# Mirror values by subtraction on VectorE and GpSimd in two of three steps, in place of a sixth product on TensorE

## Chip, cores and metric

One core of one Trainium2 chip. The metric is the device time in microseconds (us) of one execution. Medians are of 4 to 11 runs.

Engines: PE is TensorE, DVE is VectorE, ACT is ScalarE, POOL is GpSimd, SP starts most DMAs.

## The reference

A two-dimensional Fourier transform (real part only) of 8 sequences of 3008 x 256, then a gated feed-forward layer:

```python
X = np.fft.fft(x, axis=1)
X = np.fft.fft(X, axis=2)
x = X.real.astype(np.float32).reshape(B * S, D)       # 24064 x 256
gate = np.maximum(x @ w_gate, 0.0)                    # 256 x 1536
val = x @ w_val
return (gate * val @ w_out).astype(np.float32)
```

The kernel never builds the last axis of the transform: it multiplies the folded cosine and sine tables into the weights, so that a row of the transform and its mirror image share products.

## The kernel before

The work is 288 steps: 8 batches, 3 blocks of rows in each, 12 slices of 128 hidden features. For one slice, `pq[:, 0]` is the even part of the input and `pq[:, 1]` the odd part. With weights `wc` and `ws` a step makes the gate `G` and the value `V` of 512 rows. A further product with `wm` then turns each of them, in place in PSUM, into the gate and value of the 512 mirror rows. `wm` is -2 times `ws`, except in row 0, where it is 0, because that row holds a term that does not change sign. So a step has six products of 512 columns, of which two, one for `G` and one for `V`, only make the mirror rows.

```python
def plus(b, blk, f, i):            # i = 0: gate, i = 1: value
    ...
    nc.tensor.matmul(e[i][:], lhsT=wc[i][:, fs], rhs=pq[:, 0, :], start=True, stop=False)
    nc.tensor.matmul(e[i][:], lhsT=ws[i][:, fs], rhs=pq[:, 1, :], start=False, stop=True)
    if i == 0:
        e["gs"] = gp.tile([128, 512], F32, tag="gs", name="gs")
        nc.scalar.activation(e["gs"][:], e[0][:], ACTF.Relu)
    else:
        nc.vector.tensor_tensor(e["h"][:, 0, :], e["gs"][:], e[1][:], op=ALU.mult)

def minus(b, blk, f, i):
    ...
    nc.tensor.matmul(e[i][:], lhsT=wm[i][:, fs], rhs=pq[:, 1, :], start=False, stop=True,
                     skip_group_check=True)
    ...                            # gate: Relu on ScalarE; value: mirror half of h = gs * V on VectorE

for t in range(n + NF):
    for i in range(2):
        if 0 < t <= n:
            minus(*steps[t - 1], i)
        if t < n:
            plus(*steps[t], i)
    for fn in extra.get(t, ()):    # pieces of the next batch's transform, loads, folds
        fn()
    if t >= NF:
        out_piece(*steps[t - NF])  # eight output products of 256 columns
```

The "folds" are GpSimd's: they add and subtract the halves of the input of the batch after next. The issue order of each engine is the program's order.

## Time and profile before

| | before |
|---|---|
| time, median | 734.13 us |
| step without transform pieces | 2.17 us |
| from one batch to the next | 81.32 us |
| busy: PE, DVE, ACT, POOL | 92%, 63%, 52%, 30% |
| TensorE clock granted | 0.998 |

Lines of the page of the kernel before: the span; the busy us, share and instructions of each engine; the chain of waits followed back from the last instruction, as shares of the span; and three groups, each with its line, engine, operation, output<-input, shapes and count, then busy us and mean ns of one, then the idle time in front of it and who ended most of it.

```profile
span 733.5 us, 12121 instructions
...
PE 676.0 (92%) x4354; PEld 432.3 (59%) x4432; DVE 462.5 (63%) x747; ACT 381.8 (52%) x701; POOL 221.5 (30%) x116
...
PE 87%; DMA 4%; POOL 3%; DVE 3%; issue 1%; ACT 1%; SPq 0%; POOLq 0%; ACTq 0%; DVEq 0%
...
L367 DVE TENSOR_TENSOR h<-gs,V 128x512 bf16<-128x512 f32 x288 | 197.9, 687 | 215.5 <-PE V L360 161.2
...
L353 DVE TENSOR_TENSOR h<-gs,V 128x512 bf16<-128x512 f32 x288 | 195.9, 680 | 1.1 <-ACT gs L351 0.5
...
L360 PE MATMUL V<-pq,wm_92 128*128 128x512 bf16 x288 | 109.4, 380 | 4.2 <-DVE h L353 3.9
```

The chain is 87% PE. The two VectorE groups are the products gate times value of the plain rows (line 353) and of the mirror rows (line 367). The third group, 288 products into V with `wm`, is the one that the change attacks. PE's groups add up to more than its busy time, because matmuls overlap; distances between starts are the better measure. The timeline of one step (start us, duration us, engine, line, operation, count; other engines' lines and weight loads left out):

```profile
451.86 0.38 PE L360 MATMUL G<-pq,wm_91 128*128 128x512 bf16 x1
...
452.08 0.38 PE L347 MATMUL G<-pq,wc_87 128*128 128x512 bf16 x1
...
452.30 0.38 PE L348 MATMUL G<-pq,ws_89 128*128 128x512 bf16 x1
...
452.51 0.38 PE L360 MATMUL V<-pq,wm_92 128*128 128x512 bf16 x1
...
452.73 0.38 PE L347 MATMUL V<-pq,wc_88 128*128 128x512 bf16 x1
...
452.94 0.38 PE L348 MATMUL V<-pq,ws_90 128*128 128x512 bf16 x1
...
453.00 0.69 DVE L367 TENSOR_TENSOR h<-gs,V 128x512 bf16<-128x512 f32 x1 [0.92 <-PE V L360]
453.16 1.04 PE L385 MATMUL po<-wo,h 128*128 128x256 bf16 x8
...
454.03 0.38 PE L360 MATMUL G<-pq,wm_91 128*128 128x512 bf16 x1
```

A 512-column product starts every 0.21 to 0.22 us, eight output products take 0.87 us (453.16 to 454.03), and the step from one mirror gate product to the next is 454.03 - 451.86 = 2.17 us. PE has no gap. Below, "step" always means this distance.

### The profile page before, as it was taken

The numbers are of one execution on the slowest core, as the hardware profiler recorded it, in microseconds if no ns is written. First come the engines' busy times: TensorE is split into PE (matmuls) and PEld (weight loads), VectorE is DVE, ScalarE is ACT, GpSimd is POOL, SyncE is SP. The second block draws the span as 40 slices with busy tenths as digits, with TensorE's granted clock in tenths as the row PEclk, the third lists the DMA queues.
The fourth block names the chain that finished last, engine by engine and source line by source line (L and its number), as shares of the span: only waits on it lengthen the run. The fifth ranks groups of instructions, "written<-read, shape, count | busy, mean of one in ns | idle before, by whom it ended". The sixth has DMA issues, their size and how long they took to land.

```text
span 733.5 us, 12121 instructions
## 1 busy us (share of the span) xinstructions
PE 676.0 (92%) x4354; PEld 432.3 (59%) x4432; DVE 462.5 (63%) x747; ACT 381.8 (52%) x701; POOL 221.5 (30%) x116
## 2 busy tenths in 40 slices
PE   0168899899999999999999999999999999999997
PEld 0033366566666666666666666666666666666665
DVE  6613766566666766666666667666666667666661
ACT  2114555456555555555555555555555655555551
POOL 2836829202920086004910095005900000000000
PEclk9999999999999999999999999999999999999999
DMA  9467172616342544216251554135221151111213
GB/s 200 169 153 130 42 163 74 155 30 160 101 114 59 119 117 99 71 43 175 72 137 36 119 143 109 35 84 144 64 57 29 30 142 28 44 44 28 56 30 84
DMA packets 26971, 67.61 MB, mean 92 GB/s; under 512 B 3856, under 2 KB 17680, under 8 KB 24720
## 3 DMA queue, kind: packets, MB, share of 16 engines
q1 hardware_dynamic: 24340, 51.84, 27.2%
q0 software_dynamic: 2448, 13.37, 8.2%
q10 hardware_dynamic: 124, 1.64, 1.0%
q8 instruction: 34, 0.56, 0.3%
q14 instruction: 25, 0.20, 0.1%
HBM read 36.68 MB, written 30.93 MB: 92 GB/s over the span
## 4 chain that ended last, share of the span: by engine, by line
PE 87%; DMA 4%; POOL 3%; DVE 3%; issue 1%; ACT 1%; SPq 0%; POOLq 0%; ACTq 0%; DVEq 0%
PE po L385 34%; PE G L348 9%; PE V L360 9%; PE G L360 8%; PE V L347 8%; PE V L348 8%; PE G L347 7%; DMA Td<-t_256 2%; DVE h L353 1%; DMA t_969<-Td 1%; DMA t_304<-Td 1%; DMA Td<-t_719 1%; DVE q L37 0%; POOL xl L89 0%; POOL q L35 0%
## 5 line engine op out<-in xcount | busy, mean ns | idle before, releaser
L367 DVE TENSOR_TENSOR h<-gs,V 128x512 bf16<-128x512 f32 x288 | 197.9, 687 | 215.5 <-PE V L360 161.2
L364 ACT ACTIVATE gs<-G 128x512 f32<-128x512 f32 x288 | 172.2, 598 | 242.0 <-PE G L360 242.0
L385 PE MATMUL po<-wo,h 128*128 128x256 bf16 x2304 | 297.1, 273 | 0.4
L385 PEld LDWEIGHTS <-h 128*128 128x128 bf16 x2304 | 222.8, 98 | 64.5 <-issue 2.4
L353 DVE TENSOR_TENSOR h<-gs,V 128x512 bf16<-128x512 f32 x288 | 195.9, 680 | 1.1 <-ACT gs L351 0.5
L351 ACT ACTIVATE gs<-G 128x512 f32<-128x512 f32 x288 | 171.1, 594 | 0.8 <-PE G L348 0.8
L88 POOL TENSOR_TENSOR xc<-xl,xh 94x3840 f32<-94x3840 f32 (+1 forms) x8 | 60.6, 7572 | 291.0 <-DMA xl<-in_x_dram 274.7
L360 PE MATMUL V<-pq,wm_92 128*128 128x512 bf16 x288 | 109.4, 380 | 4.2 <-DVE h L353 3.9
L348 PE MATMUL G<-pq,ws_89 128*128 128x512 bf16 x282 | 107.1, 380 | 2.9 <-issue 0.2
L360 PE MATMUL G<-pq,wm_91 128*128 128x512 bf16 x288 | 109.4, 380 | 0.4 <-ACT gs L351 0.3
L347 PE MATMUL V<-pq,wc_88 128*128 128x512 bf16 x288 | 109.4, 380 | 0.0
L348 PE MATMUL V<-pq,ws_90 128*128 128x512 bf16 x267 | 101.4, 380 | 0.0
L347 PE MATMUL G<-pq,wc_87 128*128 128x512 bf16 x237 | 89.8, 379 | 0.0
L89 POOL TENSOR_TENSOR xl<-xl,xh 94x3840 f32<-94x3840 f32 (+1 forms) x8 | 60.6, 7579 | 0.6
L347 PEld LDWEIGHTS <-wc_88 128*128 128x128 bf16 x288 | 28.2, 98 | 40.0 <-issue 7.5
L391 ACT COPY os<-po 128x512 f32<-128x512 f32 x48 | 28.1, 585 | 40.6 <-PE po L385 40.6
L348 PEld LDWEIGHTS <-ws_90 128*128 128x128 bf16 x288 | 28.2, 98 | 34.2 <-issue 0.3
L348 PEld LDWEIGHTS <-ws_89 128*128 128x128 bf16 x288 | 28.2, 98 | 34.0 <-issue 0.3
L360 PEld LDWEIGHTS <-wm_92 128*128 128x128 bf16 x288 | 28.2, 98 | 34.0 <-issue 0.3
L117 PEld LDWEIGHTS <-w_82 94*96 94x96 bf16 x120 | 15.7, 131 | 50.3 <-issue 28.0
L389 DVE COPY os<-po 128x512 f32<-128x512 f32 x48 | 33.0, 688 | 6.7 <-PE po L385 6.7
L347 PEld LDWEIGHTS <-wc_87 128*128 128x128 bf16 x288 | 28.2, 98 | 5.2 <-issue 0.8
(345 smaller groups left out, 346.3 us busy)
## 6 DMA issues: line engine op xcount, KB each, us to landing
out_dram<-os SPq DMA_DIRECT2D x176, 128.0 KB, 2.1
xl<-in_x_dram SPq DMA_DIRECT2D x7, 1360.0 KB, 9.8
xl<-in_x_dram SPq DMA_DIRECT2D x7, 238.0 KB
wst_103<-in_moe_w_gate_dram SPq DMA_DIRECT2D x2, 768.0 KB, 19.6
wst_106<-in_moe_w_val_dram SPq DMA_DIRECT2D x2, 768.0 KB, 22.9
out_dram<-os SPq DMA_DIRECT2D x16, 96.0 KB, 5.2
xl<-in_x_dram ACTq DMA_DIRECT2D x1, 1360.0 KB
Td<-t_256 SPq DMA_DIRECT2D x4, 192.0 KB, 9.1
```

Of the source, the lines that this page charges most:

```text
L88: eng.tensor_tensor(c1, x1, rev, op=ALU.subtract)
L89: eng.tensor_tensor(x1, x1, rev, op=ALU.add)
L347: nc.tensor.matmul(e[i][:], lhsT=wc[i][:, fs], rhs=pq[:, 0, :], start=True, stop=False)
L348: nc.tensor.matmul(e[i][:], lhsT=ws[i][:, fs], rhs=pq[:, 1, :], start=False, stop=True)
L351: nc.scalar.activation(e["gs"][:], e[0][:], ACTF.Relu)
L353: nc.vector.tensor_tensor(e["h"][:, 0, :], e["gs"][:], e[1][:], op=ALU.mult)
L360: nc.tensor.matmul(e[i][:], lhsT=wm[i][:, fs], rhs=pq[:, 1, :], start=False, stop=True, skip_group_check=True)
L364: nc.scalar.activation(e["gs"][:], e[0][:], ACTF.Relu)
L367: nc.vector.tensor_tensor(free(e["h"][:], 512 + NB - 1, [NB, 16], [-1, NB]), e["gs"][:].rearrange("p (a k) -> p a k", k=NB), e[1][:].rearr ...
L385: nc.tensor.matmul(po[:, s % 2, :], lhsT=ht[b, blk, ff][:, sg, g * 128:(g + 1) * 128], rhs=wo[:, ff, :], start=(ff == 0), stop=(ff == NF - 1))
L389: nc.vector.tensor_copy(os_[:, s - 1:s + 1, :], po[:])
L391: nc.scalar.copy(os_[:, s - 1:s + 1, :], po[:])
```

## The change

In the mirror rows V becomes P - S + 2N, where P is the even part's product, S the odd part's, and N what row 0 alone gives. As V = P + S before that, the mirror value is 2(P + N) - V. So the change keeps an fp32 copy E = P + N, made by VectorE between the two value products (`even`), and after the second one VectorE makes 2E - V in place (`mirror_value`). The mirror half of h is then a product of two SBUF tensors, which GpSimd can make. This is done in steps with t % 3 != 2 from the second batch on: 168 of 288. N comes from a row broadcast to all partitions (`nb`) and a per-partition scalar (`af`). Other parts change with it: one PSUM bank for the transform and three for V, five gate buffers for four, all output and transform copies on ScalarE, folds in chunks of three and issued one operation per step from step 8 of a batch, the input loads moved forward to step 1, and the transform pieces two or three steps later.

The core of the diff (set-up, folds and schedule constants cut):

```diff
-    gp = ctx.enter_context(tc.tile_pool(name="gp", bufs=4, space=SB))
+    gp = ctx.enter_context(tc.tile_pool(name="gp", bufs=5, space=SB))
+    ep = ctx.enter_context(tc.tile_pool(name="ep", bufs=3, space=SB))
...
-    psv = ctx.enter_context(tc.tile_pool(name="psv", bufs=2, space=PS))
+    psv = ctx.enter_context(tc.tile_pool(name="psv", bufs=3, space=PS))
...
+    def split(t):
+        return NBLK * NF <= t < len(steps) and t % 3 != 2
...
+    def even(t):
+        b, blk, f = steps[t]
+        e = ht[t]
+        e["E"] = ep.tile([128, 512], F32, tag="e", name="E")
+        nc.vector.scalar_tensor_tensor(e["E"][:], nbt[b, blk][:], af[:, f:f + 1], e["V"][:],
+                                       op0=ALU.mult, op1=ALU.add)
...
+    def mirror_value(t):
+        b, blk, f = steps[t]
+        e = ht[t]
+        if split(t):
+            nc.vector.scalar_tensor_tensor(e["E"][:], e["E"][:], 2.0, e["V"][:], op0=ALU.mult, op1=ALU.subtract)
+            mirror_h(t, nc.gpsimd, e["E"])
         else:
+            nc.tensor.matmul(e["V"][:], lhsT=wm[1][:, f * 128:(f + 1) * 128], rhs=pqt[b, blk][:, 1, :],
+                             start=False, stop=True, skip_group_check=True)
+            mirror_h(t, nc.vector, e["V"])
...
     for t in range(n + NF):
+        if 0 < t <= n:
+            mirror_gate(t - 1)
+        if t < n:
+            gate(t)
+        if 0 < t <= n:
+            if split(t - 1):
+                value(t - 1, 1)
+            else:
+                mirror_value(t - 1)
+        if t < n and not split(t):
+            value(t, 0)
+            value(t, 1)
         for fn in extra.get(t, ()):
             fn()
         if t >= NF:
+            out_piece(t - NF, 0)
+        if split(t):
+            value(t, 0)
+            even(t)
+        if t >= NF:
+            out_piece(t - NF, 1)
+        if 0 < t <= n and split(t - 1):
+            mirror_value(t - 1)
```

`value(t, 0)` is the even product into V and `value(t, 1)` the odd one, which must not start before the even copy is made; that product is followed by the plain rows' product on VectorE.

More of the change, by code (lines that the diff above doesn't have):

```diff
@@ L1 @@
+import itertools
 import math
@@ L57 @@
     xp = ctx.enter_context(tc.tile_pool(name="xp", bufs=1, space=SB))
+    xcp = ctx.enter_context(tc.tile_pool(name="xcp", bufs=2, space=SB))
     tp = ctx.enter_context(tc.tile_pool(name="tp", bufs=2, space=SB))
-    psd = ctx.enter_context(tc.tile_pool(name="psd", bufs=2, space=PS))
+    psd = {}
     pqp = ctx.enter_context(tc.tile_pool(name="pqp", bufs=5, space=SB))
@@ L64, with run @@
     Td = [nc.dram_tensor(f"Td{b}", (8 * NKA, 16 * D), BF16, kind="Internal").ap() for b in range(B)]
+    Nd = nc.dram_tensor("Nd", (B * NBLK, 512), BF16, kind="Internal").ap()
+    def run(ops):
+        for fn in ops:
+            fn()
     xt = {}
+    XC = 3
     def load_x(b, q):
@@ L78, in load_x @@
                                      in_offset=bass.IndirectOffsetOnAxis(ap=ix[:, b:b + 1], axis=0))
-        xt[b] = (xl, xh, xp.tile([NA, J - 2, D], F32, tag="xc", name="xc"),
-                 tp.tile([NA, J, D], BF16, tag="eo", name="eo"))
+        xt[b] = (xl, xh, tp.tile([NA, J, D], BF16, tag="eo", name="eo"))
     def fold(b, eng, lo, hi):
-        xl, xh, xc, eo = xt[b]
+        xl, xh, eo = xt[b]
         n = hi - lo
-        x1, c1, e1 = xl[:, lo:hi, :], xc[:, lo - 1:hi - 1, :], eo[:, lo:hi, :]
+        x1, e1 = xl[:, lo:hi, :], eo[:, lo:hi, :]
@@ L87, in fold @@
         rev = free(xh[0:NA], (NB // 2 - lo) * D, [-D, n], [1, D])
-        eng.tensor_tensor(c1, x1, rev, op=ALU.subtract)
-        eng.tensor_tensor(x1, x1, rev, op=ALU.add)
-        eng.tensor_tensor(e1[:, :, 1:H], x1[:, :, 1:H], free(x1, D - 1, [D, n], [-1, H - 1]), op=ALU.add)
-        eng.tensor_tensor(e1[:, :, H + 1:D], c1[:, :, 1:H], free(c1, D - 1, [D, n], [-1, H - 1]), op=ALU.subtract)
-        eng.tensor_copy(free(e1, 0, [D, n], [H, 2]), free(x1, 0, [D, n], [H, 2]))
+        if lo > 0:
+            c1 = xcp.tile([NA, XC, D], F32, tag="xc", name="xc")[:, 0:n, :]
+            yield lambda: eng.tensor_tensor(c1, x1, rev, op=ALU.subtract)
+            yield lambda: eng.tensor_tensor(x1, x1, rev, op=ALU.add)
+            yield lambda: eng.tensor_tensor(e1[:, :, H + 1:D], c1[:, :, 1:H],
+                                            free(c1, D - 1, [D, n], [-1, H - 1]), op=ALU.subtract)
@@ L94, in fold_ends @@
+        yield lambda: eng.tensor_tensor(e1[:, :, 1:H], x1[:, :, 1:H], free(x1, D - 1, [D, n], [-1, H - 1]),
+                                        op=ALU.add)
     def fold_ends(b, eng):
-        xl, xh, xc, eo = xt[b]
+        xl, xh, eo = xt[b]
         for op, o in ((ALU.add, 1), (ALU.subtract, H + 1)):
-            eng.tensor_tensor(free(eo[:], o, [(J - 1) * D, 2], [1, H - 1]),
-                              free(xl[:], 1, [(J - 1) * D, 2], [1, H - 1]),
-                              free(xl[:], D - 1, [(J - 1) * D, 2], [-1, H - 1]), op=op)
@@ L100, in fold_ends, with fold_edges @@
-        eng.tensor_copy(free(eo[:], 0, [(J - 1) * D, 2], [H, 2]), free(xl[:], 0, [(J - 1) * D, 2], [H, 2]))
-    def fold_all(b):
-        fold(b, nc.gpsimd, 1, J - 1)
-        fold_ends(b, nc.gpsimd)
+            yield lambda op=op, o=o: eng.tensor_tensor(
+                free(eo[:], o, [(J - 1) * D, 2], [1, H - 1]), free(xl[:], 1, [(J - 1) * D, 2], [1, H - 1]),
+                free(xl[:], D - 1, [(J - 1) * D, 2], [-1, H - 1]), op=op)
+    def fold_edges(b, eng, lo, hi):
+        xl, xh, eo = xt[b]
+        yield lambda: eng.tensor_copy(free(eo[:, lo:hi, :], 0, [D, hi - lo], [H, 2]),
+                                      free(xl[:, lo:hi, :], 0, [D, hi - lo], [H, 2]))
@@ L106, with fold_all @@
+    def fold_all(b, eng):
+        for lo in range(1, J - 1, XC):
+            yield from fold(b, eng, lo, min(lo + XC, J - 1))
+        yield from fold_ends(b, eng)
+        yield from fold_edges(b, eng, 0, J)
     t1t = {}
@@ L110, in stage1 @@
             t1t[b] = tp.tile([96, 16, D], BF16, tag="t1", bufs=1, name="t1")
-        t1, eo = t1t[b], xt[b][3]
-        ps = psd.tile([128, 512], F32, tag="d", name="ps1")
+        t1, eo = t1t[b], xt[b][2]
+        ps = psd["now"].tile([128, 512], F32, tag="d", name="ps1")
         for i in range(2):
@@ L144, in rotate @@
         t4 = t4t[b]
-        ps = psd.tile([128, 512], F32, tag="d", name="psr")
+        ps = psd["now"].tile([128, 512], F32, tag="d", name="psr")
         nc.tensor.matmul(ps[:, 0:NKA], lhsT=rot[:], rhs=t4[:, :, H], start=True, stop=True)
         nc.vector.tensor_copy(t4[:, :, H], ps[:, 0:NKA])
-    pqt = {}
+    pqt, nbt = {}, {}
     def stage2(b, blk, cs, evac):
@@ L153, in stage2 @@
             pqt[b, blk] = pqp.tile([128, 2, 512], BF16, tag="pq", name="pq")
+            nbt[b, blk] = pqp.tile([128, 512], BF16, tag="nb", name="nb")
         t4, pq = t4t[b], pqt[b, blk]
-        ps = psd.tile([128, 512], F32, tag="d", name="ps2")
+        ps = psd["now"].tile([128, 512], F32, tag="d", name="ps2")
         for g in range(4):
@@ L162, in stage2 @@
             nc.vector.tensor_copy(pq[:, cs, :], ps[:])
+        if cs == 1:
+            row = view(Nd, (b * NBLK + blk) * 512, [[512, 1], [1, 512]])
+            nc.sync.dma_start(out=row, in_=pq[0:1, 1, :])
+            nc.sync.dma_start(out=nbt[b, blk][:], in_=view(row, 0, [[0, 128], [1, 512]]))
     ix = const.tile([96, B], I32, tag="ix")
@@ L178 @@
     wo = const.tile([128, NF, D], BF16, tag="wo")
+    af = const.tile([128, NF], F32, tag="af")
+    one = const.tile([1, 1], BF16, tag="one")
+    nc.vector.memset(one[:], 1.0)
     with tc.tile_pool(name="st", bufs=1, space=SB) as st, \
          tc.tile_pool(name="sp", bufs=2, space=SB) as sp, \
+         tc.tile_pool(name="psd0", bufs=2, space=PS) as psd0, \
          tc.tile_pool(name="psw", bufs=4, space=PS) as psw:
+        psd["now"] = psd0
         wst = []
@@ L291 @@
         pl.tensor_scalar(s2[:], pf[:], scalar1=1.0, scalar2=-2.0, op0=ALU.min, op1=ALU.mult)
-        fold(0, nc.vector, 2, 8)
-        fold(0, nc.vector, 8, 12)
-        fold(0, nc.gpsimd, 12, 16)
-        fold_ends(0, nc.vector)
-        fold(0, nc.vector, 1, 2)
+        for lo, hi in ((2, 5), (5, 8), (8, 10), (10, 12)):
+            run(fold(0, nc.vector, lo, hi))
+            run(fold_edges(0, nc.vector, lo, hi))
+        for lo, hi in ((12, 14), (14, 16)):
+            run(fold(0, nc.gpsimd, lo, hi))
+        run(fold_edges(0, nc.gpsimd, 12, 16))
+        run(fold_ends(0, nc.vector))
+        run(fold(0, nc.vector, 1, 2))
+        run(fold_edges(0, nc.vector, 0, 2))
+        run(fold_edges(0, nc.vector, 16, 17))
         for k, c in enumerate((1, 2, 3, 4, 5, 6, 7, 0)):
@@ L305 @@
             shuffle_in(0, 4 * blk, 4 * blk + 4)
-        fold_all(1)
+        run(fold_all(1, nc.gpsimd))
         for n in range(DF // 512):
@@ L320 @@
                         nc.scalar.activation(wm[i][:, sl_], ps[:], ACTF.Copy, scale=s2[:])
-    rotate(0)
-    for blk in range(NBLK):
-        stage2(0, blk, 0, "act")
-        stage2(0, blk, 1, "dve")
-    gp = ctx.enter_context(tc.tile_pool(name="gp", bufs=4, space=SB))
+        ps = psw.tile([128, 512], F32, tag="w", name="psn")
+        for f in range(NF):
+            nc.tensor.matmul(ps[:, f:f + 1], lhsT=ws[1][0:1, f * 128:(f + 1) * 128], rhs=one[:],
+                             start=True, stop=True)
+        nc.vector.tensor_copy(af[:], ps[:, 0:NF])
+        rotate(0)
+        for blk in range(NBLK):
+            stage2(0, blk, 0, "act")
+            stage2(0, blk, 1, "dve")
+    gp = ctx.enter_context(tc.tile_pool(name="gp", bufs=5, space=SB))
+    ep = ctx.enter_context(tc.tile_pool(name="ep", bufs=3, space=SB))
     hp = ctx.enter_context(tc.tile_pool(name="hp", bufs=2 * NF + 1, space=SB))
-    op = ctx.enter_context(tc.tile_pool(name="op", bufs=4, space=SB))
+    op = ctx.enter_context(tc.tile_pool(name="op", bufs=3, space=SB))
+    psd["now"] = ctx.enter_context(tc.tile_pool(name="psd", bufs=1, space=PS))
     psg = ctx.enter_context(tc.tile_pool(name="psg", bufs=2, space=PS))
-    psv = ctx.enter_context(tc.tile_pool(name="psv", bufs=2, space=PS))
+    psv = ctx.enter_context(tc.tile_pool(name="psv", bufs=3, space=PS))
     pso = ctx.enter_context(tc.tile_pool(name="pso", bufs=2, space=PS))
@@ L336 @@
     ht = {}
-    def plus(b, blk, f, i):
-        pq = pqt[b, blk]
-        fs = slice(f * 128, (f + 1) * 128)
-        if i == 0:
-            ht[b, blk, f] = {"h": hp.tile([128, 2, 512], BF16, tag="h", name="h"),
-                             0: psg.tile([128, 512], F32, tag="g", name="G"),
-                             1: psv.tile([128, 512], F32, tag="v", name="V")}
-        e = ht[b, blk, f]
-        nc.tensor.matmul(e[i][:], lhsT=wc[i][:, fs], rhs=pq[:, 0, :], start=True, stop=False)
-        nc.tensor.matmul(e[i][:], lhsT=ws[i][:, fs], rhs=pq[:, 1, :], start=False, stop=True)
-        if i == 0:
-            e["gs"] = gp.tile([128, 512], F32, tag="gs", name="gs")
-            nc.scalar.activation(e["gs"][:], e[0][:], ACTF.Relu)
-        else:
-            nc.vector.tensor_tensor(e["h"][:, 0, :], e["gs"][:], e[1][:], op=ALU.mult)
@@ L355, in minus @@
-    def minus(b, blk, f, i):
-        pq = pqt[b, blk]
-        fs = slice(f * 128, (f + 1) * 128)
-        e = ht[b, blk, f]
-        nc.tensor.matmul(e[i][:], lhsT=wm[i][:, fs], rhs=pq[:, 1, :], start=False, stop=True,
-                         skip_group_check=True)
-        if i == 0:
-            e["gs"] = gp.tile([128, 512], F32, tag="gs", name="gs")
-            nc.scalar.activation(e["gs"][:], e[0][:], ACTF.Relu)
-        else:
-            nc.vector.tensor_tensor(free(e["h"][:], 512 + NB - 1, [NB, 16], [-1, NB]),
-                                    e["gs"][:].rearrange("p (a k) -> p a k", k=NB),
-                                    e[1][:].rearrange("p (a k) -> p a k", k=NB), op=ALU.mult)
-            ht[b, blk, f] = e["h"]
+    def split(t):
+        return NBLK * NF <= t < len(steps) and t % 3 != 2
@@ new lines, in gate @@
+    def gate(t):
+        b, blk, f = steps[t]
+        pq, fs = pqt[b, blk], slice(f * 128, (f + 1) * 128)
+        e = ht[t] = {"h": hp.tile([128, 2, 512], BF16, tag="h", name="h"),
+                     "G": psg.tile([128, 512], F32, tag="g", name="G"),
+                     "gs": gp.tile([128, 512], F32, tag="gs", name="gs")}
+        nc.tensor.matmul(e["G"][:], lhsT=wc[0][:, fs], rhs=pq[:, 0, :], start=True, stop=False)
+        nc.tensor.matmul(e["G"][:], lhsT=ws[0][:, fs], rhs=pq[:, 1, :], start=False, stop=True)
+        nc.scalar.activation(e["gs"][:], e["G"][:], ACTF.Relu)
@@ new lines, in mirror_gate, with value @@
+    def mirror_gate(t):
+        b, blk, f = steps[t]
+        e = ht[t]
+        nc.tensor.matmul(e["G"][:], lhsT=wm[0][:, f * 128:(f + 1) * 128], rhs=pqt[b, blk][:, 1, :],
+                         start=False, stop=True, skip_group_check=True)
+        e["gm"] = gp.tile([128, 512], F32, tag="gs", name="gm")
+        nc.scalar.activation(e["gm"][:], e["G"][:], ACTF.Relu)
+    def value(t, part):
+        b, blk, f = steps[t]
+        e, pq, fs = ht[t], pqt[b, blk], slice(f * 128, (f + 1) * 128)
+        if part == 0:
+            e["V"] = psv.tile([128, 512], F32, tag="v", name="V")
+            nc.tensor.matmul(e["V"][:], lhsT=wc[1][:, fs], rhs=pq[:, 0, :], start=True, stop=split(t))
+        else:
+            nc.tensor.matmul(e["V"][:], lhsT=ws[1][:, fs], rhs=pq[:, 1, :], start=False, stop=True,
+                             skip_group_check=split(t))
+            nc.vector.tensor_tensor(e["h"][:, 0, :], e["gs"][:], e["V"][:], op=ALU.mult)
@@ new lines, in even, with mirror_h @@
+    def even(t):
+        b, blk, f = steps[t]
+        e = ht[t]
+        e["E"] = ep.tile([128, 512], F32, tag="e", name="E")
+        nc.vector.scalar_tensor_tensor(e["E"][:], nbt[b, blk][:], af[:, f:f + 1], e["V"][:],
+                                       op0=ALU.mult, op1=ALU.add)
+    def mirror_h(t, eng, val):
+        e = ht[t]
+        eng.tensor_tensor(free(e["h"][:], 512 + NB - 1, [NB, 16], [-1, NB]),
+                          e["gm"][:].rearrange("p (a k) -> p a k", k=NB),
+                          val[:].rearrange("p (a k) -> p a k", k=NB), op=ALU.mult)
@@ L372, with out_piece @@
+    def mirror_value(t):
+        b, blk, f = steps[t]
+        e = ht[t]
+        if split(t):
+            nc.vector.scalar_tensor_tensor(e["E"][:], e["E"][:], 2.0, e["V"][:], op0=ALU.mult, op1=ALU.subtract)
+            mirror_h(t, nc.gpsimd, e["E"])
+        else:
+            nc.tensor.matmul(e["V"][:], lhsT=wm[1][:, f * 128:(f + 1) * 128], rhs=pqt[b, blk][:, 1, :],
+                             start=False, stop=True, skip_group_check=True)
+            mirror_h(t, nc.vector, e["V"])
     state = {}
-    def out_piece(b, blk, f):
-        for k in range(8 * f, 8 * f + 8):
+    def out_piece(t, half):
+        b, blk, f = steps[t]
+        for k in range(8 * f + 4 * half, 8 * f + 4 * half + 4):
@@ L384, in out_piece @@
             po, os_ = state["po"], state["os"]
-            nc.tensor.matmul(po[:, s % 2, :], lhsT=ht[b, blk, ff][:, sg, g * 128:(g + 1) * 128],
+            nc.tensor.matmul(po[:, s % 2, :], lhsT=ht[t - f + ff]["h"][:, sg, g * 128:(g + 1) * 128],
                              rhs=wo[:, ff, :], start=(ff == 0), stop=(ff == NF - 1))
             if s % 2 == 1 and ff == NF - 1:
-                if s == 1:
-                    nc.vector.tensor_copy(os_[:, s - 1:s + 1, :], po[:])
-                else:
-                    nc.scalar.copy(os_[:, s - 1:s + 1, :], po[:])
+                nc.scalar.copy(os_[:, s - 1:s + 1, :], po[:])
             if s == 3 and ff == NF - 1:
@@ L416 @@
         t0 = b * NBLK * NF
-        tl, t1, tr, t2, d2 = (17, 16, 28, 29, 1) if b == 0 else (10, 4, 19, 20, 2)
+        tl, tf, t1, tr, d2 = (17, 18, 16, 28, 1) if b == 0 else (1, 8, 6, 22, 2)
         if b + 2 < B:
             at(t0 + tl, load_x, b + 2, nc.sync)
-            at(t0 + tl + 1, fold_all, b + 2)
+            at(t0 + tf, lambda b=b: folds.insert(0, fold_all(b + 2, nc.gpsimd)))
         if b + 1 < B:
             for c in range(8):
-                at(t0 + t1 + c, stage1, b + 1, c, "act" if c % 2 else "dve")
+                at(t0 + t1 + c, stage1, b + 1, c, "act")
             at(t0 + t1 + 8, shuffle_out, b + 1, 0, 8)
@@ L427 @@
             for i in range(6):
-                at(t0 + t2 + d2 * i, stage2, b + 1, i // 2, i % 2, "dve" if i % 2 else "act")
+                at(t0 + tr + 1 + d2 * i, stage2, b + 1, i // 2, i % 2, "act")
+    folds = []
     n = len(steps)
     for t in range(n + NF):
-        for i in range(2):
-            if 0 < t <= n:
-                minus(*steps[t - 1], i)
-            if t < n:
-                plus(*steps[t], i)
+        if 0 < t <= n:
[10 more added lines that the diff above has]
+            value(t, 1)
         for fn in extra.get(t, ()):
@@ L439 @@
         if t >= NF:
-            b, blk, f = steps[t - NF]
-            out_piece(b, blk, f)
+            out_piece(t - NF, 0)
[6 more added lines that the diff above has]
+            mirror_value(t - 1)
+        if folds:
+            for fn in itertools.islice(folds[0], 3 if t < NBLK * NF else 1):
+                fn()
 _INS = ['x', 'moe_w_gate', 'moe_w_val', 'moe_w_out']
```

## The prediction

> **What bounds it now.** TensorE. The page gives PE 92% busy at a clock of 0.98 to 1.00; the chain of waits is 87% PE. Busy times overlap, so I use start-to-start distances from the timeline at 400 us: a 512-column matmul every 0.217 us, eight output matmuls in 0.87 us, so a step of 6 x 0.217 + 0.87 = 2.17 us without a gap. 36 steps plus transform products make the 81.3 us between batches. By stretches, VectorE is 66% busy, ScalarE 56%, GpSimd 30%.
>
> **Removed.** 168 of 288 steps (two of three from the second batch on) lose the mirror value product: 168 x 0.217 = 36.4 us, all on the critical path. Three steps fall from 6.50 to 6.08 us.
>
> **Added.** A split step gives VectorE two scalar-tensor-tensor operations of 512 fp32 elements with one PSUM input. The existing ones take 0.68 to 0.69 us; a per-partition scalar cost about 0.06 us elsewhere (0.353 against 0.29 us for 128x256), so I estimate 0.75 and 0.69 us. It loses the mirror product there, half the output copies and the stage copies (to ScalarE). Per three steps it works 5.5 of 6.08 us: nearly full, but it fits. GpSimd gets 168 mirror products of 128x512. From its folds (8.32 us for 3840 elements, 2.33 for 1024: 2.13 ns per element plus 0.15) I estimate 1.25 us each. It cannot read PSUM (Trainium skill, "GPSIMD Engine Reference", Engine selection), hence the fp32 copy. ScalarE rises to about 75%.
>
> **Where it may be lost.**
> 1. The loop through the even copy: VectorE starts 0.49 us after the start of the matmul it waits for (timeline), works 0.75, releases PE about 0.05 later: 1.29 us. PE has 0.217 + 0.435 + 0.65 = 1.30 us of other work before the second value product. No slack: 0 to 0.06 us lost per split step, my estimate 4 us in all.
> 2. GpSimd while it folds (23 operations, one per step, batches 2 to 6). Three steps cost it 2 x 1.27 + 3 x 1.41 = 6.8 us against PE's 6.08 (6.7 with transform products). Its lag holds the five gate buffers, so ScalarE and then PE wait. Slack is about 1.1 us; I estimate 1 to 3 us lost per batch, 9 in all. The first fold waits in order for its loads (17 us after issue before; about 16 us ahead now).
> 3. The prologue: folds in smaller pieces, about 1 us on the chain to the first transform.
>
> VectorE and GpSimd should not block each other: each VectorE operation has one SBUF tensor, and the Trainium skill ("SBUF — State Buffer", Who interferes with whom) says such an instruction does not contend. The trace agrees: the mirror product takes 688 ns with GpSimd idle (590 to 660 us) and with it busy (179 to 202 us).
>
> **Time.** 734.2 - 36.4 + 4 + 9 + 1 = about 711; the losses overlap in part, so 708 us. Range 697 to 720. Chances: faster by over 2% 0.89, within 2% 0.09, slower 0.02.
>
> **What would show it.** The mirror value group on PE falls from 288 to 120. Later batches take 76 us without fold losses, 77 to 79 with. The even copy takes 0.72 to 0.78 us, the mirror value 0.68 to 0.70, the GpSimd product 1.2 to 1.3. VectorE is about 85% busy later, GpSimd over 90% while it folds. PE's waits on the even copy are under 0.1 us each; ScalarE waits on GpSimd only in fold stretches.
>
> **What would make it wrong.** A GpSimd product near 1.6 us (about +20 us); a scalar-tensor-tensor over 0.8 us (+10 us or more); a port conflict through the scalar pointer; fold data landing late. If GpSimd's products are under 1.1 us and the loop closes, about 699 us.

## The result, and the profile after

| | before | after |
|---|---|---|
| time, median | 734.13 us (733.79 to 734.46) | 706.88 us (706.05 to 710.02) |
| ratio, 95% interval | | 0.9637 (0.9606 to 0.9668) |
| first batch | 81.42 us | 79.95 us |
| batches 2 to 6 (with folds) | 81.32 us | 77.41 us |
| batch 7 (transform pieces, no fold) | 81.32 us | 76.93 us |
| 35 steps of batch 8 (neither) | 75.90 us | 72.30 us |

A ratio here and below is the mean time of one kernel's runs over that of the kernel before in the same rounds, so it is not quite the ratio of the medians. Batches are measured in the one profiled execution of each kernel, from the start of a batch's first mirror gate product to the next batch's.

The lines of the page after that answer to those shown above:

```profile
span 705.8 us, 12357 instructions
...
PE 646.8 (92%) x4198; PEld 415.8 (59%) x4276; DVE 519.0 (74%) x830; ACT 428.5 (61%) x798; POOL 448.3 (64%) x393
...
PE 72%; POOL 12%; issue 5%; DVE 4%; DMA 4%; ACT 1%; SPq 0%; DVEq 0%; POOLq 0%
...
L423 POOL TENSOR_TENSOR h<-gm,E 128x512 bf16<-128x512 f32 x168 | 213.9, 1273 | 190.5 <-DVE E L431 169.9
...
L411 DVE TENSOR_TENSOR h<-gs,V 128x512 bf16<-128x512 f32 x288 | 190.3, 684 | 51.0 <-PE V L409 47.7
...
L417 DVE SCALAR_TENSOR_TENSOR E<-nb,af,V 128x512 f32<-128x512 bf16 x168 | 125.3, 746 | 7.0 <-PE V L407 3.6
L431 DVE SCALAR_TENSOR_TENSOR E<-E,V 128x512 f32<-128x512 f32 x168 | 114.3, 680 | 0.0
...
L434 PE MATMUL V<-pq,wm_91 128*128 128x512 bf16 x120 | 45.5, 379 | 3.9 <-DVE h L411 3.9
```

V's products with `wm` fell from 288 to 120. The even copy (line 417) takes 746 ns, 2E - V (line 431) 680, GpSimd's product (line 423) 1273. The chain is now 72% PE, and GpSimd's products and folds stand in it. Two stretches of a middle batch (length, then busy us and instruction count of PE, weight loads, DVE, ACT and POOL, then the granted clock, DMA share, GB/s), the first with folds and the second without:

```profile
247.00:280.00 33.00, 32.79 (x221) 21.69 (x223) 27.10 (x44) 22.42 (x42) 31.72 (x24) 1.00 0.33 95
...
300.00:308.00 8.00, 7.95 (x56) 5.30 (x56) 6.50 (x11) 5.61 (x11) 3.69 (x4) 1.00 0.12 32
```

GpSimd is 96% busy (31.72 of 33 us) in the first and 46% in the second; VectorE about 82% in both. PE has hardly a visible gap, which shows how little its busy share tells: the losses below hide under the matmuls' modelled ends, and starts have to be compared.

Without any wait a batch would save 24 x 0.217 = 5.2 us. Batches 2 to 6 save 3.9. The steps of the last batch, which has neither transform nor fold, repeat with a period of three: 2.07, 2.17, 1.95 us. By count they should be 1.95, 2.17, 1.95 (the second holds six products of 512 columns, the others five). One step of three loses 0.115 us. The timeline around it (lines left out at "..."):

```profile
639.81 0.38 PE L397 MATMUL G<-pq,wm_90 128*128 128x512 bf16 x1
...
640.01 0.58 ACT L455 COPY os<-po 128x512 f32<-128x512 f32 x1 [0.81 <-PE po L452]
...
640.46 0.38 PE L434 MATMUL V<-pq,wm_91 128*128 128x512 bf16 x1
...
640.49 0.60 ACT L400 ACTIVATE gm<-G 128x512 f32<-128x512 f32 x1
...
641.11 0.38 PE L407 MATMUL V<-pq,wc_87 128*128 128x512 bf16 x1
...
641.13 0.69 DVE L423 TENSOR_TENSOR h<-gm,V 128x512 bf16<-128x512 f32 x1 [0.47 <-ACT gm L400]
...
641.73 0.74 DVE L417 SCALAR_TENSOR_TENSOR E<-nb,af,V 128x512 f32<-128x512 bf16 x1
641.76 0.38 PE L397 MATMUL G<-pq,wm_90 128*128 128x512 bf16 x1
...
642.20 0.38 PE L391 MATMUL G<-pq,ws_88 128*128 128x512 bf16 x1
...
642.53 0.38 PE L409 MATMUL V<-pq,ws_89 128*128 128x512 bf16 x1
...
643.83 0.38 PE L397 MATMUL G<-pq,wm_90 128*128 128x512 bf16 x1
...
646.00 0.38 PE L397 MATMUL G<-pq,wm_90 128*128 128x512 bf16 x1
```

Read it backwards. The second value product (line 409, 642.53) follows the gate product of line 391 by 0.33 us, not by 0.21 or 0.22: it waited for the even copy (line 417), which started at 641.73. That copy could have started at about 641.60, 0.49 us after its matmul (line 407, 641.11), as VectorE does elsewhere after a matmul. It queued behind the mirror product of the unsplit step in front (line 423 on DVE, 641.13; the copy starts 0.60 us after it), which waited not for its value (line 434, 640.46, so ready about 640.95) but for ScalarE's gate (line 400, 640.49 to 641.09). And the gate ran that late because ScalarE was still copying outputs (line 455, from 640.01). Four engines are in this chain, and each link looks harmless.

The second loss is seen once in each of batches 2 to 6 (2.54 us at the 24th step in place of 1.95; the next then 2.17 in place of 2.29). Around it:

```profile
276.70 1.83 POOL L98 TENSOR_TENSOR xc<-xl,xh 94x768 f32<-94x768 f32 x1
...
278.61 1.82 POOL L99 TENSOR_TENSOR xl<-xl,xh 94x768 f32<-94x768 f32 x1
...
280.39 1.27 POOL L423 TENSOR_TENSOR h<-gm,E 128x512 bf16<-128x512 f32 x1
...
281.69 0.60 ACT L392 ACTIVATE gs<-G 128x512 f32<-128x512 f32 x1 [0.60 <-POOL h L423]
...
282.34 0.38 PE L397 MATMUL G<-pq,wm_90 128*128 128x512 bf16 x1 [0.42 <-ACT gs L392]
```

GpSimd works through two fold operations, so a mirror product (280.39) is late; ScalarE needs the gate buffer that this product holds and waits 0.60 us; PE then waits 0.42 us for ScalarE. Batch 7, which has the same transform pieces and no fold, is 0.48 us shorter.

The account from the two traces, in us: 36.4 removed; 0.8 lost to the order in each of batches 2 to 7 (5.2 - 4.4, read from batch 7, and confirmed by e1 and e4 below, where batch 7 saves all of the 5.2) and 1.4 in the last, together 6.2; 5 x 0.48 = 2.4 lost to the folds; the first batch 1.5 shorter, the steps' start 1.2 later. That is 28.1 net, and the spans differ by 733.5 - 705.8 = 27.7.

The last two items are partly chance. After short gaps PE ran at half its clock for about 3 us: right at the first step in the profiled run after, in the first batch's transform in that of the kernel before. One stretch of each, the first of the kernel after, the second of the kernel before (with the counts in brackets left out, the sixth number after the stretch's length, here 0.50, is the granted clock):

```profile
71.30:74.40 3.10, 2.86 (x7) 1.07 (x9) 0.69 (x1) 1.19 (x2) 3.02 (x3) 0.50 0.24 69
```

```profile
134.00:136.00 2.00, 1.96 (x7) 0.84 (x7) 0.69 (x1) 1.04 (x2) 0.00 (x0) 0.50 1.05 262
```

The 512-column products in such a stretch mostly start 0.42 to 0.43 us apart in place of 0.22. By an estimate from the traces it costs about 1.0 us at the first step (the transform's start to the tenth step takes 22.2 to 22.5 us in the eight traces with it, 21.3 to 21.4 in the four other traces of the changed kernel and its variants) and 1.6 in the first batch (81.2 and 81.4 us in e9 and e8, which have it there alone, 79.5 and 79.8 in e7 and e3). The traces of e3 and e7 show none at either place, so it may be a part of the spread of 4 us among the runs of the kernel after; only the profiled executions can show that.

### The profile page after: what moved, and what is told of

The parts are those of the page before. It is cut to its first block, busy times and chain, and to the rows that moved or that the text cites. A ratio compares the mean times of both kernels' runs of the same rounds, so it can differ in the third digit from the quotient of the medians.

```text
span 705.8 us, 12357 instructions
## 1 busy us (share of the span) xinstructions
PE 646.8 (92%) x4198; PEld 415.8 (59%) x4276; DVE 519.0 (74%) x830; ACT 428.5 (61%) x798; POOL 448.3 (64%) x393
## 4 chain that ended last, share of the span: by engine, by line
PE 72%; POOL 12%; issue 5%; DVE 4%; DMA 4%; ACT 1%; SPq 0%; DVEq 0%; POOLq 0%
PE po L452 28%; PE G L391 8%; PE V L409 7%; PE G L397 7%; PE V L407 6%; POOL h L423 6%; PE G L390 6%; PE V L434 3%; PE psw L346 3%; DMA xh<-in_x_dram,ix 3%; POOL xl L99 2%; POOL xc L98 2%; POOL eo L102 1%; DVE h L411 1%; POOL eo L100 1%
## 5 line engine op out<-in xcount | busy, mean ns | idle before, releaser
L423 POOL TENSOR_TENSOR h<-gm,E 128x512 bf16<-128x512 f32 x168 | 213.9, 1273 | 190.5 <-DVE E L431 169.9
L400 ACT ACTIVATE gm<-G 128x512 f32<-128x512 f32 x288 | 172.6, 599 | 140.1 <-PE G L397 140.1
L411 DVE TENSOR_TENSOR h<-gs,V 128x512 bf16<-128x512 f32 x288 | 190.3, 684 | 51.0 <-PE V L409 47.7
L392 ACT ACTIVATE gs<-G 128x512 f32<-128x512 f32 x288 | 171.8, 596 | 5.3 <-POOL h L423 3.0
L423 DVE TENSOR_TENSOR h<-gm,V 128x512 bf16<-128x512 f32 x120 | 82.6, 688 | 75.2 <-ACT gm L400 52.6
L417 DVE SCALAR_TENSOR_TENSOR E<-nb,af,V 128x512 f32<-128x512 bf16 x168 | 125.3, 746 | 7.0 <-PE V L407 3.6
L431 DVE SCALAR_TENSOR_TENSOR E<-E,V 128x512 f32<-128x512 f32 x168 | 114.3, 680 | 0.0
L409 PE MATMUL V<-pq,ws_89 128*128 128x512 bf16 x280 | 106.2, 379 | 0.1
L407 PE MATMUL V<-pq,wc_87 128*128 128x512 bf16 x263 | 100.0, 380 | 0.2 <-issue 0.2
L98 POOL TENSOR_TENSOR xc<-xl,xh 94x768 f32<-94x768 f32 (+1 forms) x37 | 66.0, 1784 | 34.7 <-DMA xh<-in_x_dram,ix 18.0
L99 POOL TENSOR_TENSOR xl<-xl,xh 94x768 f32<-94x768 f32 (+1 forms) x37 | 66.0, 1782 | 1.7
L434 PE MATMUL V<-pq,wm_91 128*128 128x512 bf16 x120 | 45.5, 379 | 3.9 <-DVE h L411 3.9
```

Source lines behind the costliest of these rows:

```text
L392: nc.scalar.activation(e["gs"][:], e["G"][:], ACTF.Relu)
L400: nc.scalar.activation(e["gm"][:], e["G"][:], ACTF.Relu)
L407: nc.tensor.matmul(e["V"][:], lhsT=wc[1][:, fs], rhs=pq[:, 0, :], start=True, stop=split(t))
L409: nc.tensor.matmul(e["V"][:], lhsT=ws[1][:, fs], rhs=pq[:, 1, :], start=False, stop=True, skip_group_check=split(t))
L411: nc.vector.tensor_tensor(e["h"][:, 0, :], e["gs"][:], e["V"][:], op=ALU.mult)
L417: nc.vector.scalar_tensor_tensor(e["E"][:], nbt[b, blk][:], af[:, f:f + 1], e["V"][:], op0=ALU.mult, op1=ALU.add)
```

## The experiments

Theory A: the 0.115 us in every third step come from the order on VectorE (the even copy behind a mirror product that waits for ScalarE), and GpSimd's lag while it folds costs 0.48 us per fold batch through the gate buffers. Theory B, the rival and the first item of my prediction: the loop from the first value product through the even copy to the second value product is too long by itself. A second rival: the prediction's 9 us for the folds.

| run | median us | ratio | step pattern, last batch | batches 2-6, 7, 8 |
|---|---|---|---|---|
| kernel after | 706.88 | 0.9637 | 2.07 2.17 1.95 | 77.41, 76.93, 72.30 |
| e1_even_first | 704.80 | 0.9600 | 1.95 2.17 1.95 | 77.01 (one 77.37), 76.14, 71.27 |
| e2_copy_late | 708.59 | 0.9644 | 1.95 2.17 1.95 | 77.0 to 77.9, 76.14, 70.93 |
| e3_gate_bufs7 | 705.52 | 0.9607 | 2.07 2.17 1.95 | 76.93, 76.94, 72.29 |
| e4_order_and_bufs | 700.04 | 0.9536 | 1.95 2.17 1.95 | 76.14 to 76.49, 76.14, 71.27 |
| e5_no_split | 736.75 | 1.0026 | 2.17 2.17 2.17 | 81.32, 81.32, 75.89 |
| e7_three_of_four | 702.72 | 0.9567 | 1.95 1.95 1.95 2.17 | 76.45 to 77.47, 75.55, 70.91 |
| e8_no_pointer | 705.73 | 0.9604 | 2.01 2.17 1.95 | 77.11, 76.51, 71.55 |
| e9_copy_late_from_2nd | 706.21 | 0.9611 | 1.95 2.17 1.95 | 77.0 to 77.45, 76.14, 70.93 |
| e10_rotate_29 | 698.55 | 0.9497 | 1.95 2.17 1.95 | 76.14 to 76.48, 76.14, 71.27 |
| e12_cut_3_5 | 707.55 | 0.9622 | 2.07 2.17 1.95 | 77.33, 76.94, 72.29 |
| e13_order_cut_5_3 | 717.74 | 0.9759 | 2.06 2.27 1.95 | 78.6 to 79.0, 78.58, 73.73 |

All had five rounds. All are correct but e8.

### e1_even_first

```diff
         else:
             nc.tensor.matmul(e["V"][:], lhsT=wm[1]...)
-            mirror_h(t, nc.vector, e["V"])
+            if split(t + 1):
+                late.append(t)
+            else:
+                mirror_h(t, nc.vector, e["V"])
...
             even(t)
+            while late:
+                mirror_h(late[0], nc.vector, ht[late.pop(0)]["V"])
```

> Edit: on VectorE the even copy of a split step is issued before the mirror product of the unsplit step in front of it, not after. Theory A (order): in every third step the even copy starts 0.13 us late because it queues behind that mirror product, which itself waits for ScalarE's gate; TensorE then waits 0.115 us. So the 2.07 us steps become 1.95 us, and about 6 us go (706.9 to about 701); but a shorter period gives GpSimd less time while it folds, so its stall (0.5 us per fold batch now) may grow to about 1.3 us and eat up to 4 us of it: 700 to 705. The last batch, which has no fold, goes from 72.3 to about 70.9 us. Theory B (the loop even copy to second product is too long by itself, as item 1 of the prediction has it): steps stay at 2.07 us, 706 to 708.

Measured: 704.80 us (703.62 to 706.86). The 2.07 us steps are 1.95, and batch 7 fell by 0.8 us and batch 8 by 1.0. Batches 2 to 6 gained only 0.4: ScalarE's waits for GpSimd grew, in total from 3.0 us to 3.8 plus 2.8 behind a fold. So the order is one cause, and curing it alone hands half of its gain to the folds. Batch 8 was expected at 70.9; one of its steps was 2.30 us in place of 1.95, because an even copy started 0.36 us late with no wait on record that explains it (the profile names an output product that the program issues after the copy). The same slip stands at the same step in e4, e10 and e13. What it is stays open.

### e2_copy_late and e9_copy_late_from_2nd

```diff
-                nc.scalar.copy(os_[:, s - 1:s + 1, :], po[:])
+                held.append(lambda po=po, os_=os_, s=s: nc.scalar.copy(os_[:, s - 1:s + 1, :], po[:]))
             if s == 3 and ff == NF - 1:
-                store(b, blk, sg, os_)
+                held.append(lambda b=b, blk=blk, sg=sg, os_=os_: store(b, blk, sg, os_))
...
             gate(t)
+        while held:
+            held.pop(0)()
```

e9 does the same only for outputs of the second batch and later.

> Edit: ScalarE's output copies (and the stores behind them) are issued one step later, behind the two gate activations; VectorE's order is as in the changed kernel. Theory A says the mirror product waited for a gate activation that ran 0.19 us late behind such a copy, so taking the copy out of the way cures the same 0.115 us: 2.07 us steps become 1.95, 700 to 705 in all, as in e1. Theory A' (VectorE's order alone matters, not ScalarE's): no change, 706 to 708. Theory B: no change.

> Edit: e2 (late output copies) for the outputs of the second and later batches only; the first batch's copies and stores go out as in the changed kernel. Theory: e2 cured the 2.07 us steps (its trace says 1.95) but its stores, one step later on the queue, held up the first batch's transform shuffle, where the trace shows a wait of 3.6 us instead of 1.8 and slow matmuls after it; without that, the first batch is back at about 80 us and the whole at 703 to 705.5. Rival (late copies cost something in every batch): 707 to 709 as e2.

Measured: e2 708.59 us, e9 706.21. The step pattern was cured in both (1.95), with VectorE's order untouched: so ScalarE's copy is a link of the chain, as Theory A has it, and Theories A' and B fall. The totals missed: both lie above the 700 to 705 and 703 to 705.5 expected. In e2's trace the first batch takes 83.41 us; its stores were one step later in the queue ahead of the transform's shuffle, and PE's wait for it (us in total, times, longest us) doubled from the 1.8 us that it is in the kernel after; half-clock matmuls came on top:

```profile
PE psr L163 <- DMA t<-Td: 3.6, 1, 3.6
```

In e9 that wait is back at 2.0 us, but this execution had half-clock matmuls after it (first batch 81.23 us), and the fold losses had grown to 0.9 us or more per batch. So e9's total is not clear of the kernel after, though its step pattern is; that both totals missed for these reasons is read from one trace each.

### e3_gate_bufs7 and e4_order_and_bufs

```diff
-    gp = ctx.enter_context(tc.tile_pool(name="gp", bufs=5, space=SB))
+    gp = ctx.enter_context(tc.tile_pool(name="gp", bufs=7, space=SB))
```

e4 is this together with e1.

> Edit: seven gate buffers instead of five, nothing else. Theory A: only the stall of 0.6 us at one step of each of the five fold batches goes (ScalarE waiting for GpSimd to free a gate buffer): those batches fall from 77.41 to 76.93 us, 2.4 us in all, to about 704.5; the 2.07 us steps stay. Rival (my prediction as written, 9 us lost to GpSimd's lag): 698 to 700.

> Edit: e1 and e3 together. Theory A: both losses go: 706.9 - 6.2 - 2.4 = about 698.3 us, batches of about 76.1 us with or without folds, the last 70.9. If the two losses overlap or GpSimd cannot keep up even with seven buffers: 700 to 703.

Measured: e3 705.52 us; batches 2 to 6 are 76.93 us, exactly batch 7, and ScalarE no longer waits for GpSimd in the steps. So the folds cost 2.4 us there, not 9, and all through the gate buffers; the median fell by 1.4 us, within the spread of the runs. e4: 700.04 us (698.82 to 702.85), 6.8 less than the kernel after where 8.6 was expected; batch 7 is 76.14, and batches 2 to 6 either 76.14 or, with one slip as above, 76.49. Against e1, 4.8 us go to the two buffers, against 1.4 in e3 (in batches 2 to 6 of the profiled executions 4.0 against 2.4): with the order mended, buffers are worth more. e4's timeline at the place that was shown for the kernel after:

```profile
639.17 0.38 PE L397 MATMUL G<-pq,wm 128*128 128x512 bf16 x1
...
639.85 0.60 ACT L400 ACTIVATE gm<-G 128x512 f32<-128x512 f32 x1
...
640.47 0.38 PE L407 MATMUL V<-pq,wc 128*128 128x512 bf16 x1
...
640.97 0.75 DVE L417 SCALAR_TENSOR_TENSOR E<-nb,af,V 128x512 f32<-128x512 bf16 x1 [0.95 <-PE V L407]
...
641.12 0.38 PE L397 MATMUL G<-pq,wm 128*128 128x512 bf16 x1
...
641.63 0.68 DVE L423 TENSOR_TENSOR h<-gm,V 128x512 bf16<-128x512 f32 x1
641.77 0.38 PE L409 MATMUL V<-pq,ws 128*128 128x512 bf16 x1
```

The even copy (line 417) now starts 0.50 us after its matmul (line 407), the mirror product (line 423) follows it, and the second value product (641.77) comes 0.65 us after line 397's product, as three products should.

### e12_cut_3_5 and e13_order_cut_5_3

```diff
-        for k in range(8 * f + 4 * half, 8 * f + 4 * half + 4):
+        for k in range(8 * f + 3 * half, 8 * f + (3, 8)[half]):     # e12; on the kernel after
+        for k in range(8 * f + 5 * half, 8 * f + (5, 8)[half]):     # e13; on e4
```

> Edit: the changed kernel, with the eight output products of a step cut 3 and 5 instead of 4 and 4 around the first value product. TensorE then has 0.109 us more work between the first value product and the second. Theory A (in every third step the even copy's start is set by the mirror product before it, which waits for ScalarE, and not by the first value product): an earlier first value product does not help, the steps stay at 2.06 to 2.07 us and the time at 706 to 708. Theory B (the loop from the first value product through the even copy is too long): 2.07 becomes 1.95 to 1.97 and the time 700 to 703.

> Edit: e4 with the output products cut 5 and 3: 0.109 us less work of TensorE between the two value products. If the loop has no slack once the order is mended (0.49 + 0.75 + 0.05 = 1.29 against 1.30 us of other work, the prediction's item 1), nearly all of it shows in each of the 168 split steps: 1.95 us steps become about 2.05, and 700.0 becomes 713 to 718. If the loop has slack of 0.1 us: 700 to 702.

Measured: e12 707.55 us, the steps still 2.07: an earlier first value product does nothing, so Theory B falls for the kernel after. e13 717.74 us, and the second value product of each of the two split slices of a period comes 0.10 us late (that of the second slice falls in the 2.17 us step, which becomes 2.27). Taking 0.109 us from PE's other work cost 17.7 us by medians, taken in different rounds, and 17.0 in batches 2 to 8 of the profiled executions, which is 168 x 0.10. So the loop has next to no slack, as the prediction's first item said, but in e4 it closes. A loop in e13's timeline, from the first value product through the even copy to the second:

```profile
650.08 0.38 PE L407 MATMUL V<-pq,wc 128*128 128x512 bf16 x1
...
650.56 0.75 DVE L417 SCALAR_TENSOR_TENSOR E<-nb,af,V 128x512 f32<-128x512 bf16 x1 [1.04 <-issue]
...
651.36 0.38 PE L409 MATMUL V<-pq,ws 128*128 128x512 bf16 x1
```

0.48 us to the copy's start, 0.75 of copy, 0.05 to the second product: 1.28 us against the predicted 1.29.

### e8_no_pointer

```diff
-        nc.vector.scalar_tensor_tensor(e["E"][:], nbt[b, blk][:], af[:, f:f + 1], e["V"][:],
+        nc.vector.scalar_tensor_tensor(e["E"][:], nbt[b, blk][:], 1.0, e["V"][:],
```

> Edit: the changed kernel with the constant 1.0 in place of the per-partition scalar in the even copy; the result is wrong on purpose. The even copy should fall from 0.746 to 0.68 to 0.69 us. Theory A and the loop: the late even copies of every third step end 0.06 us earlier, so 2.07 us steps become about 2.01 and 3 us go: 703 to 705. If the even copy does not shorten, nothing changes; if the wait of TensorE does not hang on the even copy's end, 2.07 us steps stay with a shorter copy.

The even copy's group in this run (mean ns after the busy us):

```profile
L417 DVE SCALAR_TENSOR_TENSOR E<-nb,V 128x512 f32<-128x512 bf16 x168 | 115.1, 685 | 6.4 <-PE V L407 5.6
```

The copy fell from 746 to 685 ns, and the 2.07 us steps to 2.01: the 0.06 us passed to PE one for one, in the one step of three where the copy is late. PE's wait hangs on the end of this copy. The median, 705.73, is 0.7 above the range; this profiled run had a half-clock stretch in the first batch (81.41 us), and the later batches gained as expected (0.30, 0.42, 0.75). The result is wrong by 0.098.

### e5_no_split

```diff
-        return NBLK * NF <= t < len(steps) and t % 3 != 2
+        return False
```

> Edit: no step is split; everything else of the change stays (issue order, one transform bank and three value banks, output copies on ScalarE, chunked folds, the broadcast rows that nobody reads). Theory: the rest of the change is neutral (the trace of the changed kernel has the first batch 1.5 us shorter and the steps' start 1.2 us later), so 733 to 736, and the whole gain comes from the 168 removed products less their waits. Rival (the rest has a gain or a cost of its own, above all moving copies from VectorE to ScalarE): outside 730 to 738.

Measured: 736.75 us, ratio 1.0026 (1.0011 to 1.0042): a little slower than before, and 0.75 above the theory's range. All batches after the first take 81.32 us, exactly as before, so the other edits gain nothing in those batches. In the profiled execution the first step comes 1.4 us later than in the kernel before and the first batch is 0.6 us shorter; the rest of the 2 us is not located. Moving copies from VectorE to ScalarE was worth nothing by itself. The split is then worth 736.75 - 706.88 = 29.9 us by medians of different rounds, or 28.6 by the ratios (1.0026 - 0.9637 of 734).

### e7_three_of_four

```diff
-        return NBLK * NF <= t < len(steps) and t % 3 != 2           # on e4
+        return NBLK * NF <= t < len(steps) and t % 4 != 3
```

> Edit: e4 (order and seven gate buffers) with three of four steps split instead of two of three: 21 more products gone, 4.5 us. Theory (GpSimd's capacity while it folds sets the ratio): four steps cost GpSimd 3 x 1.27 + 4 folds of about 1.4 = 9.4 us against TensorE's 8.0, so each of the five fold batches loses some us and the whole is slower than e4: 703 to 718; the batches without folds gain 0.6 us or more. Rival (only the order on VectorE mattered): about 695.5.

Measured: 702.72 us, slower than e4 (and 0.3 below the range given). Batches 7 and 8, without folds, gained 0.6 and 0.4; batches 2 to 6 lost up to 1.3. ScalarE's waits for GpSimd, which e4 has none of in its steps, are back in spite of seven buffers:

```profile
ACT gs L392 <- POOL h L423: 12.1, 12, 1.2
```

There is a second path in this trace: at one or two steps of each fold batch the even copy starts 0.15 to 0.19 us later than its usual 0.50 after its matmul, behind a GpSimd product; of GpSimd it can only await its E buffer, and there are three. So GpSimd's time while it folds sets the ratio of split steps, not VectorE's: in batch 7, without folds, VectorE kept up, and 0.6 us of the 0.65 that three products are worth came through.

### e10_rotate_29

```diff
-        tl, tf, t1, tr, d2 = (17, 18, 16, 28, 1) if b == 0 else (1, 8, 6, 22, 2)    # on e4
+        tl, tf, t1, tr, d2 = (17, 18, 16, 29, 1) if b == 0 else (1, 8, 6, 22, 2)
```

> Edit: e4, and the first batch's transform goes on one step later (29 instead of 28), where its data has landed. TensorE's one wait of about 2 us on the shuffle there goes (2.1 us in e4's trace), and with it the chance of a stretch of slow matmuls after the idle time: 697 to 699 against e4's 700.0. If the wait only moves by a step: 700.

Measured: 698.55 us (698.34 to 698.84), ratio 0.9497. The wait is gone, the first batch 78.28 us against 80.14, and the runs spread over 0.5 us in place of 4 (this trace, too, has a half-clock stretch, at the first step). This is the fastest version: 37 us under the kernel before in the same rounds, 8 under the kernel after by medians.

## Why the prediction was right

The time was: 708 predicted, 706.88 measured. Point by point:

- **What was removed** held: 168 products, 36.4 us on the critical path. e5 shows that from the second batch on nothing else in the change gains.
- **Costs of the new operations** held: 746, 680 and 1273 ns against 0.75, 0.69 and 1.25 us. The Trainium skill ("GPSIMD Engine Reference", Engine selection) has two-input operations on GpSimd about twice as slow as on VectorE; here 1273 against 688 ns, a factor of 1.85, so the trace about agrees.
- **No port conflict** held. The Trainium skill ("SBUF — State Buffer", Who interferes with whom) says that a VectorE instruction with at most one SBUF input, outside the 2-port modes, does not contend with GpSimd. The trace after agrees: from 150 us on, the 50 even copies during which GpSimd did nothing took 747 ns on average, the 78 that its work covered for over 80% of their length 745. Its scalar pointer does not matter to that.
- **The loop (item 1)**: its length and its lack of slack were right (e13), and its loss was put at 4 us. The loss was 6.2 us, and not for the loop's length: the even copy queued behind a mirror product held up by ScalarE's copy (e1, e2 and e12). I had priced VectorE's share of a period, not the order within it. The term was mis-sized, and its cause misnamed. PE's waits were also not "under 0.1 us each" but 0.115 in one split step of two and none in the other.
- **The folds (item 2)**: the mechanism was right, down to ScalarE waiting for gate buffers and only in fold batches (e3), but the size, 9 us, was off: 2.4. The pace was right (GpSimd 96% busy), but the lag came late: in batch 3 GpSimd's product follows 2E - V by at most 0.5 us until the 14th step, and by 2.15 at the 23rd, just before the stall. That transform pieces in the early steps and a PE slowed by the order loss kept it short is argued; for the second, e1 speaks. Once the order is mended it is worth more (e1: 0.9 per batch; e4 against e1: 4.8, or 4.0 by batches). The first fold's loads were in time; no wait for them appears after the first batch.
- **The prologue (item 3)**: the first step came 1.2 us later, near the 1 us predicted, but by luck, for it was not on the chain named. The first batch's transform went on at 67.26 us against 67.48 before; what came after it, a wait of 0.79 us for the last transform copy and half-clock matmuls, made the 1.2.
- **Smaller signs**: later batches without folds were to take 76 us and took 76.9; those with folds 77 to 79 and took 77.4. VectorE was to be about 85% busy and was 82; ScalarE 75% and was about 70.

So the total came out well partly by luck, because two errors offset each other: 2.2 us too little for the order, 6.6 too much for the folds. The prediction's sum is 711.8, not 711, so its discount for overlap was 3.8. That the losses overlap was right: in a fold batch the order alone costs 0.79 us (e3 against e4's 76.14), the folds alone 0.87 (e1), both together 1.27 (kernel after), which is 0.4 less than the sum, 2.0 in five batches.

## What to carry to other kernels

When an engine goes from two thirds full to over 80%, as VectorE here from 66% to 82%, price the order of its queue, not only its sum: an operation that a bottleneck waits for must not stand behind one that waits for a third engine. A loop across engines that closes with no slack (0.48 + 0.75 + 0.05 us against 1.30) works, but the 0.1 us put into it in e13 came out on the bottleneck once per split step. And mend overlapping losses together: in a fold batch the order alone gave 0.40 us (e1), the buffers alone 0.48 (e3), both 1.27 (e4); the medians of the whole, with their spread, fell by 2.1, 1.4 and 6.8.

## What the Trainium skill lacked or had wrong

- "TensorE: Matmul & The Clock Gate" (Part 1, and its closing table) puts the half clock after an idle window of about 3.4 us and advises against gaps of over about 3 us. Here the granted clock was 0.50 for 3.1 us (71.3 to 74.4 us, kernel after) although the longest wait of PE in the 5 us before was 0.79 us (several waits and short products: PE was busy 58% of 66.0 to 71.3 us), and it was 0.50 in 134 to 136 us of the kernel before, after a wait of 1.95 us. The trace of e3, which has the same code there, kept its full clock; so it can come after gaps shorter than this rule names, and need not. Elsewhere the page allows for short, frequent idles; what set it off here stays open.
- "VectorE: DVE Perf Modes" gives no time for scalar-tensor-tensor. With 512 fp32 elements and one PSUM input it took 680 ns with a constant, like a plain product (684 to 688), and 746 with a per-partition scalar; putting a constant there brought 685 (e8).
- None of the pages cited here has the hand-over times on which such loops turn: VectorE started 0.48 to 0.50 us after the start of the 512-column matmul that it waited for, and TensorE 0.05 us after VectorE's end.
